# Block sums of the second weight matrix made by loads that add to SBUF, two VectorE additions in place of four

## The chip, the cores and the metric

One core of one Trainium2 chip. The metric is the device time of one execution in microseconds, the median of several runs. TensorE (PE) multiplies, with weight loads (PEld) beside the products; VectorE (DVE), ScalarE (ACT) and GpSimd (POOL) work element by element; SyncE (SP) and GpSimd issue most DMAs. Each engine takes its instructions in order.

## The reference

The kernel computes a block of a transformer on `x` of 2048 tokens by 512 channels: a linear attention, added to `x`, and then a token-mixing MLP, added again:

```python
x = A_x
h = x + _A_ref(_layernorm(x), A_wqkv, A_w_phi, A_wo)
# _B_ref(z), with z = layernorm(h); S = 2048, D = 512, F = 1792
u = gelu(einsum("bsd,sf->bdf", layernorm(z), w1) + b1)
y = einsum("bdf,fs->bds", u, w2) + b2
h2 = h + y.transpose(0, 2, 1)
```

The change lies in the second MLP product, `y`, with `w2` of 1792 by 2048 in float32.

## The kernel before, in words

The attention and the first MLP product (`w1`, weights split in a high and a low float32r part, lines 663 and 670, three products each, lines 66 to 68) end at about 375 us. The second product runs from there to the end.

It is done by blocks with a scheme of the Strassen kind: each 256 by 256 block of `w2` and the matching block of U are cut in 2 by 2, and 7 products of sums of sub-blocks replace 8. The sums on U's side (`operands_u`) are made once and kept in `UB`; those on the side of the weights are made as the weights stream in.

- A *step* is one pair of output tiles `sp` (0 to 7) and one block row `p` (0 to 6); there are 56 steps in the order of `STEPS`, 7 to a pair. `pair_of_tiles(sp, p)` issues the products of a step: `wide` (lines 921 and 924) and `narrow` (line 913).
- A *group* is two steps (`GRP`), 28 in all. For each there is a tile `wraw` with 7 slots of 128 columns a step. Two DMAs from SyncE (line 852), one a step, 256 KB each, fill slots 0 to 3 with the four sub-blocks. Four VectorE operations (lines 854 to 857) put the sums in slots 4, 5, 0 and 6. There are four such tiles in turn: a group's load waits until the group four before it has been split.
- `w2_parts` splits the seven slots: ScalarE writes the high part `whi`, VectorE the low part `wlo` (line 875). There are three such pairs of tiles, so the parts of group g wait for the steps of group g - 3.
- `in_order` fixes the program's order on VectorE, ScalarE and TensorE as it is written; it adds no waits. `stream_w2(n)` runs behind step n and every second step issues the parts of the group two ahead and the sums of the group four ahead. Behind the next to last step of a pair nothing is issued; it comes behind the pair's last step instead, after that step's end sums.
- At the last step of a pair, the products are in six PSUM banks: `b16`, `b7`, `b5`, `b4`, which the next pair writes again, and `b3`, `b2`, which alternate with another two. ScalarE and VectorE (lines 979 to 989) sum them into `ot` and `low`. GpSimd then issues three accumulating stores of 256 KB into `out`: two from `ot` (line 991), and one from `low` (line 992) into rows that the second also adds to, so it waits for that one to land.
- The first five groups are loaded, and two split, while the first product still runs (from 266.9 us).

The table `P1` to `P7` names for each of the 7 products the slot of the weights and the operand of U.

Of the kernel before, what the change touches and what calls it, by code (L numbers as in the profile page):

```python
# [12 lines left out]
ALU = mybir.AluOpType  # L13
# [4 lines left out]
P = 128  # L18
# [19 lines left out]
def block_kernel(ctx: ExitStack, tc: tile.TileContext, x, xT, wT, phic, wo, w1, b1, w2, b2,  # L38
                 kvmask, ident_in, out):
    nc = tc.nc  # L40
# [18 lines left out]
    def split(hi, lo, src, lo_engine):  # L59

        nc.scalar.activation(hi, src, AF.Copy)
        lo_engine.tensor_sub(lo, src, hi)
# [15 lines left out]
    sums = wqp.tile([P, SUMS, NPR, 2, 2], F32, name="smq")  # L78
# [576 lines left out]
    w2v = w2.rearrange("(k p) s -> p k s", p=P)  # L655
# [125 lines left out]
    NP = NF // 2  # L781
# [52 lines left out]
    STEPS = [(sp, p) for sp in range(NT // 2) for p in range(NP)]  # L834
    GRP = 2
    AW, RAW = {}, {}
    QUEUE = {}

    def in_order(*ops):

        for op in ops:
            with ExitStack() as st:
                for ins in QUEUE.values():
                    st.enter_context(tc.issue_after(ins))
                ins = op().ins
            QUEUE[ins.engine] = ins

    def w2_sums(g):
        other = g > AHEAD + 2 and g % 4 == 1
        raw = RAW[g] = (hp if other else ws).tile([P, GRP, 7, P], F32, name="wraw", bufs=1 if other else 3)  # L850
        for i, (sp, p) in enumerate(STEPS[g * GRP:(g + 1) * GRP]):
            nc.sync.dma_start(raw[:, i, 0:4].rearrange("p (k i) s -> p k (i s)", k=2),
                              w2v[:, 2 * p:2 * p + 2, sp * 2 * P:(sp + 1) * 2 * P])
        sums = (lambda: nc.vector.tensor_add(raw[:, :, 4], raw[:, :, 0], raw[:, :, 2]),
                lambda: nc.vector.tensor_sub(raw[:, :, 5], raw[:, :, 4], raw[:, :, 1]),
                lambda: nc.vector.tensor_sub(raw[:, :, 0], raw[:, :, 1], raw[:, :, 0]),
                lambda: nc.vector.tensor_sub(raw[:, :, 6], raw[:, :, 3], raw[:, :, 5]))
        if g < AHEAD:
            with tc.issue_after(LO[-18]):
                for op in sums:  # L860
                    op()
        else:
            in_order(*sums)

    def w2_parts(g):
        home = hp if g % 3 == 2 else ws
        wh_ = home.tile([P, GRP, 7, P], F32R, name="whi")
        wl_ = home.tile([P, GRP, 7, P], F32R, name="wlo")
        for i, step in enumerate(STEPS[g * GRP:(g + 1) * GRP]):
            AW[step] = wh_[:, i], wl_[:, i]  # L870
        raw = RAW.pop(g)
        if g < AHEAD:
            split(wh_, wl_, raw, nc.vector)
        else:
            in_order(lambda: nc.scalar.activation(wh_, raw, AF.Copy), lambda: nc.vector.tensor_sub(wl_, raw, wh_))  # L875

    AHEAD = 2
    for g in range(AHEAD):
        w2_sums(g)
        w2_parts(g)  # L880
    for g in range(AHEAD, AHEAD + 2):
        w2_sums(g)
    parts_next, sums_next = [], []

    def stream_w2(n):

        if (n + 1) % NP == 0:
            for g in sums_next:
                w2_sums(g)
            sums_next.clear()  # L890
        if n % GRP == 0:
            parts_next.append(n // GRP + AHEAD)
        if (n + 2) % NP == 0:
            return
        for g in parts_next:
            if g * GRP < len(STEPS):
                w2_parts(g)
            if (g + 2) * GRP < len(STEPS):
                if (n + 3) % NP == 0:
                    sums_next.append(g + 2)  # L900
                else:
                    w2_sums(g + 2)
        parts_next.clear()


    P1, P2, P3, P4, P5, P6, P7 = (1, 1), (3, 3), (6, 2), (2, 6), (4, 4), (5, 5), (0, 0)

    def narrow(o, ps, m, sp, opens, closes):

# [20 lines left out]
    def new_bank(pool):  # L930
        return pool.tile([P, 2, HD], F32, name="py", tag="pu")

    def pair_of_tiles(sp, p):
        t = 2 * sp
        if p == 0:
            b3, b2 = [new_bank((ps_f, ps_q)[sp % 2]) for _ in range(2)]
            BK[:] = [new_bank(ps_b) for _ in range(4)] + [b3, b2]
        b16, b7, b5, b4, b3, b2 = BK
        end = p == NP - 1
        if t + 2 == NT:  # L940
            if p < NP - 3 or end:
                ps = [p - 2, p - 1, p] if end else [p]
                places = [(b16[:, 0], P1, True), (b16[:, 1], P6, False), (b7[:, 0], P7, True), (b5[:, 0], P5, True),
                          (b4[:, 0], P4, True), (b3[:, 0], P3, True), (b2[:, 0], P2, True)]
                for o, m, opens in places if end else places[5:] + places[:5]:
                    narrow(o, ps, m, sp, opens, True)
                if end:
                    last_sums(t, HB)
            return
        w3, w2, w7, w5, w4 = (b3, P3), (b2, P2), (b7, P7), (b5, P5), (b4, P4)  # L950
        if p == 0:
            wide(sp, p, w3, w2)
        elif not end:
            wide(sp, p, w3, w2, w7, w5, w4)
        narrow(b16[:, 0], [p], P1, sp, True, True)
        narrow(b16[:, 1], [p], P6, sp, False, True)
        if p == 0:
            wide(sp, p, w7, w5, w4)
        if not end:
            return  # L960
        wide(sp, p, w7)
        wide(sp, p, w5, w4)
        wide(sp, p, w3, w2)
        e = uo.tile([P, 2, HD], F32, name="e")
        u2 = uo.tile([P, HD], F32, name="u2", bufs=1)
        u3 = uo.tile([P, HD], F32, name="u3")
        ot = uo.tile([P, 2, 2, HD], F32, name="ot", bufs=1)
        low = hp.tile([P, 2, HD], F32, name="low")
        l5 = hp.tile([P, HD], F32, name="l5")

        def tile_sum(i, k, o, add):
            return lambda: nc.vector.scalar_tensor_tensor(ot[:, i, k], o, b2s[:, t + i:t + i + 1], add,  # L972
                                                          op0=ALU.add, op1=ALU.add)

        def low_sum(o, a):
            return lambda: nc.vector.tensor_add(o, a[:, 1], o)


        in_order(lambda: nc.scalar.activation(e[:, 1], b16[:, 0], AF.Copy),
                 lambda: nc.scalar.activation(l5, b5[:, 1], AF.Copy),  # L980
                 lambda: nc.vector.tensor_add(u2, b16[:, 1], e[:, 1]),
                 lambda: nc.vector.tensor_add(u3, b7[:, 0], u2), low_sum(u3, b7),
                 tile_sum(0, 1, b4[:, 0], u3),
                 lambda: nc.vector.tensor_add(l5, b5[:, 0], l5),
                 low_sum(ot[:, 0, 1], b4),
                 lambda: nc.vector.tensor_add(e[:, 0], l5, u2),
                 lambda: nc.scalar.activation(low[:, 0], b3[:, 1], AF.Copy),
                 lambda: nc.scalar.activation(low[:, 1], b2[:, 1], AF.Copy),
                 tile_sum(0, 0, l5, u3), tile_sum(1, 0, b3[:, 0], e[:, 0]), tile_sum(1, 1, b2[:, 0], e[:, 1]))
        for i in range(2):  # L990
            nc.gpsimd.dma_start(out[(t + i) * P:(t + i + 1) * P, :], flat(ot[:, i]), accum_op=ALU.add)  # L991
        nc.gpsimd.dma_start(out[(t + 1) * P:(t + 2) * P, :], flat(low), accum_op=ALU.add)
# [9 lines left out]
    def last_sums(t, hb):  # L1002
        b16, b7, b5, b4, b3, b2 = BK
        e = uo.tile([P, 2, HD], F32, name="e")
        u2 = uo.tile([P, HD], F32, name="u2", bufs=1)
        u3 = uo.tile([P, HD], F32, name="u3")
        add = nc.vector.tensor_add
        nc.scalar.activation(e[:, 1], b16[:, 0], AF.Copy)
        in_order(lambda: add(u2, b16[:, 1], e[:, 1]),
                 lambda: add(hb[1][:, 0], u2, hb[1][:, 0]),  # L1010
                 lambda: add(hb[1][:, 1], e[:, 1], hb[1][:, 1]),
                 lambda: add(u3, b7[:, 0], u2),
                 lambda: add(hb[0], hb[0], u3.unsqueeze(1).to_broadcast([P, 2, HD])),
                 lambda: add(hb[0][:, 0], b5[:, 0], hb[0][:, 0]),
                 lambda: add(hb[1][:, 0], b5[:, 0], hb[1][:, 0]),
                 lambda: add(hb[0][:, 1], b4[:, 0], hb[0][:, 1]))
        nc.sync.dma_start(out[t * P:(t + 1) * P, :], flat(hb[0]))
        for k, o, q in ((0, b3, nc.scalar), (1, b2, nc.sync)):
            in_order(lambda: add(hb[1][:, k], o[:, 0], hb[1][:, k]))
            q.dma_start(out[(t + 1) * P:NT * P, k * HD:(k + 1) * HD], hb[1][:, k])  # L1020
# [54 lines left out]
```

## Time and profile before

| what | us |
|---|---|
| median of 3 runs | 519.54 (519.3 to 520.09) |
| span of the profiled execution, first to last instruction | 517.9 |
| TensorE busy | 513.2 (99%) |
| VectorE busy | 395.0 (76%) |
| ScalarE busy | 285.3 (55%) |
| GpSimd busy | 235.9 (46%) |
| second product, from the first `py` product to the end | 375.5 to 517.9 |

The span lies 1.6 us below the median; no other time of the profiled execution is on its page. The granted TensorE clock is 1.00 throughout. How to read rows: a timeline row has start, duration, engine, line, operation, `out<-in`, and in brackets the idle time before it and what ended it. Rows of a tile have minimum, median and maximum in ns. "To landing" is the time from a DMA's issue to its last byte's arrival. Busy times of TensorE overlap from one product to the next, so starts are what is compared.

### The profile page before, as it was taken

The numbers are of one execution on the slowest core, as the hardware profiler recorded it, in microseconds if no ns is written. First come the engines' busy times: TensorE is split into PE (matmuls) and PEld (weight loads), VectorE is DVE, ScalarE is ACT, GpSimd is POOL, SyncE is SP. The second block draws the span as 40 slices with busy tenths as digits, with TensorE's granted clock in tenths as the row PEclk, the third lists the DMA queues.
The fourth block names the chain that finished last, engine by engine and source line by source line (L and its number), as shares of the span: only waits on it lengthen the run. The fifth ranks groups of instructions, "written<-read, shape, count | busy, mean of one in ns | idle before, by whom it ended". The sixth has DMA issues, their size and how long they took to land.

```text
span 517.9 us, 9772 instructions
## 1 busy us (share of the span) xinstructions
PE 513.2 (99%) x3761; PEld 434.0 (84%) x3761; DVE 395.0 (76%) x719; ACT 285.3 (55%) x501; POOL 235.9 (46%) x182
## 2 busy tenths in 40 slices
PE   9999999999999999999999999999999999999997
PEld 8888888888887777777788888888899999999997
DVE  6799889989987899697336624625797899888993
ACT  6999853526267877767756423425464434433530
POOL 3579997876999999974224000000001102110210
PEclk9999999999999999999999999999999999999999
DMA  8642301021302334333255433532134586557732
GB/s 311 209 142 84 102 22 42 1 83 44 122 27 97 103 103 119 107 103 123 82 163 162 123 94 90 184 102 62 41 115 94 141 201 136 139 156 181 137 48 61
DMA packets 46493, 57.66 MB, mean 111 GB/s; under 512 B 4080, under 2 KB 33136, under 8 KB 46448
## 3 DMA queue, kind: packets, MB, share of 16 engines
q1 hardware_dynamic: 43136, 51.38, 31.4%
q0 software_dynamic: 3024, 5.51, 7.6%
q8 instruction: 29, 0.48, 0.4%
q10 hardware_dynamic: 288, 0.17, 0.1%
q14 instruction: 16, 0.13, 0.1%
HBM read 46.81 MB, written 10.22 MB: 110 GB/s over the span
## 4 chain that ended last, share of the span: by engine, by line
PE 97%; DVE 1%; ACT 1%; issue 0%; DVEq 0%
PE pu L66 13%; PE pu L68 12%; PE pu L67 12%; PE py L921 11%; PE py L913 10%; PE py L924 6%; PE po L66 3%; PE pk_ps L66 3%; PE po L68 3%; PE po L67 3%; PE pk_ps L67 3%; PE pk_ps L68 3%; PE pv L67 3%; PE pv L66 3%; PE pv L68 3%; PE tr L591 2%
## 5 line engine op out<-in xcount | busy, mean ns | idle before, releaser
L991 POOL DMA_DIRECT2D out<-ot x14 | 12.5, 941 | 170.3 <-DVE ot L972 170.3
L66 PE MATMUL pu<-hs,whi 128*128 128x512 f32 x224 | 87.7, 394 | 0.0
L67 PE MATMUL pu<-hs,whi 128*128 128x512 f32 x224 | 87.2, 389 | 0.0
L68 PE MATMUL pu<-hs,wlo 128*128 128x512 f32 x224 | 86.5, 389 | 0.0
L670 DVE TENSOR_TENSOR wlo<-wraw,whi 128x512 fp32r<-128x512 f32 x56 | 46.9, 841 | 46.5 <-ACT whi L663 46.2
L875 ACT ACTIVATE whi<-wraw 128x1792 fp32r<-128x1792 f32 x26 | 44.0, 1704 | 30.9 <-issue 17.4
L663 ACT ACTIVATE whi<-wraw 128x512 fp32r<-128x512 f32 x56 | 34.6, 625 | 44.4 <-PE pu L67 39.4
L875 DVE TENSOR_TENSOR wlo<-wraw,whi 128x1792 fp32r<-128x1792 f32 x26 | 52.4, 2019 | 0.0
L66 PEld LDWEIGHTS pu<-hs,whi 128*128 128x128 f32 x224 | 42.0, 188 | 9.1 <-ACT hj L641 0.2
L68 PEld LDWEIGHTS pu<-hs,wlo 128*128 128x128 f32 x224 | 42.0, 188 | 8.9
L67 PEld LDWEIGHTS pu<-hs,whi 128*128 128x128 f32 x224 | 42.1, 188 | 8.5
L921 PE MATMUL py<-uf,whi 128*128 128x512 f32 x175 | 48.4, 395 | 0.0
L484 POOL TENSOR_TENSOR ez<-eq,zB 128x1024 f32<-128x1024 f32 x16 | 38.4, 2405 | 3.8 <-ACT zB L544 3.8
L913 PE MATMUL py<-uf,whi 128*128 128x256 f32 x210 | 39.0, 283 | 0.0
L213 POOL TENSOR_TENSOR pk<-pk,sk 128x1024 f32<-128x1024 f32 x16 | 31.1, 1949 | 11.2 <-DVE sk L212 10.0
L508 POOL TENSOR_TENSOR eq<-eq,w 128x1024 f32<-128x1024 f32 x16 | 32.4, 2026 | 3.2 <-DVE w L505 3.2
L921 PEld LDWEIGHTS py<-uf,whi 128*128 128x128 f32 x175 | 30.1, 189 | 3.9
L913 PEld LDWEIGHTS py<-uf,whi 128*128 128x128 f32 x210 | 32.8, 192 | 0.0
L217 POOL TENSOR_TENSOR zacc<-zacc,pk 128x1024 f32<-128x1024 f32 x13 | 31.4, 2412 | 0.5
L924 PEld LDWEIGHTS py<-uf,wlo 128*128 128x128 f32 x175 | 27.1, 189 | 3.8
L913 PE MATMUL py<-uf,wlo 128*128 128x256 f32 x105 | 29.7, 283 | 0.0
L924 PE MATMUL py<-uf,wlo 128*128 128x256 f32 x175 | 28.7, 281 | 0.0
(200 smaller groups left out, 1303.9 us busy)
## 6 DMA issues: line engine op xcount, KB each, us to landing
wraw<-in_w SPq DMA_DIRECT2D x112, 256.0 KB, 3.0
xraw<-in_xT SPq DMA_DIRECT2D x16, 256.0 KB, 2.9
xh<-in_x SPq DMA_DIRECT2D x16, 256.0 KB, 2.6
h<-in_x SPq DMA_DIRECT2D x16, 256.0 KB, 2.7
out<-h SPq DMA_DIRECT2D x16, 256.0 KB, 2.1
out<-ot POOLq DMA_DIRECT2D x14, 256.0 KB, 4.4
wraw<-in_wT SPq DMA_DIRECT2D x12, 256.0 KB, 5.1
out<-low POOLq DMA_DIRECT2D x7, 256.0 KB, 4.2
```

The lines of the kernel that those rows point to most:

```text
L66: nc.tensor.matmul(o, ah, bh, start=first, stop=False)
L67: nc.tensor.matmul(o, ah, bl, start=False, stop=False)
L68: return nc.tensor.matmul(o, al, bh, start=False, stop=last).ins
L217: nc.gpsimd.tensor_add(zacc, zacc, PK[t])
L484: nc.gpsimd.tensor_mul(EZ[t], EQ[t], zB)
L508: nc.gpsimd.tensor_mul(heads(EQ[t]), heads(EQ[t]), W[t].rearrange("p g c h -> p (g c h)").unsqueeze(2).to_broadcast([P, 2 * H, DH]))
L663: nc.scalar.activation(wh_, raw, AF.Copy)
L670: LO.append(nc.vector.tensor_sub(wl_, raw, wh_).ins)
L875: in_order(lambda: nc.scalar.activation(wh_, raw, AF.Copy), lambda: nc.vector.tensor_sub(wl_, raw, wh_))
L913: in_order(lambda: nc.tensor.matmul(o, x[:, m[0]], UB[p, m[1]][:, y], start=opens and p == 0 and i == 0, stop=closes and p == NP - 1 and i ...
L921: in_order(lambda: nc.tensor.matmul(o, wh_[:, m[0]], UB[p, m[1]], start=p == 0, stop=False, skip_group_check=True))
L924: in_order(lambda: nc.tensor.matmul(o[:, 0], wl_[:, m[0]], UB[p, m[1]][:, 0], start=False, stop=p == NP - 1, skip_group_check=True))
```

## The change

Slots are used differently: the four sub-blocks go to slots 1 to 4 (one DMA a step), and a second plain DMA copies the third of them (64 KB a step) to slot 0. When both have landed, GpSimd issues for each step a DMA that adds 128 columns by two of `w2` (128 KB) to slots 0 and 1. Two of the block sums come about in this way. VectorE makes the other two (slots 5 and 6), both additions. Some products thereby have the opposite sign, and the end sums subtract where they added. `w2_load(g)` is split from `w2_sums(g)`: loads are issued for the group five ahead of the current step's group, sums now directly before the parts of the group ahead of them. The number and shapes of TensorE's products stay as they are.

```diff
-    def w2_sums(g):
+    def w2_load(g):
+        if g * GRP >= len(STEPS):
+            return
         other = g > AHEAD + 2 and g % 4 == 1
         raw = RAW[g] = (hp if other else ws).tile([P, GRP, 7, P], F32, name="wraw", bufs=1 if other else 3)
         for i, (sp, p) in enumerate(STEPS[g * GRP:(g + 1) * GRP]):
-            nc.sync.dma_start(raw[:, i, 0:4].rearrange("p (k i) s -> p k (i s)", k=2),
-                              w2v[:, 2 * p:2 * p + 2, sp * 2 * P:(sp + 1) * 2 * P])
-        sums = (lambda: nc.vector.tensor_add(raw[:, :, 4], raw[:, :, 0], raw[:, :, 2]),
-                lambda: nc.vector.tensor_sub(raw[:, :, 5], raw[:, :, 4], raw[:, :, 1]),
-                lambda: nc.vector.tensor_sub(raw[:, :, 0], raw[:, :, 1], raw[:, :, 0]),
-                lambda: nc.vector.tensor_sub(raw[:, :, 6], raw[:, :, 3], raw[:, :, 5]))
+            cols = sp * 2 * P
+            nc.sync.dma_start(raw[:, i, 1:5].rearrange("p (k i) s -> p k (i s)", k=2),
+                              w2v[:, 2 * p:2 * p + 2, cols:cols + 2 * P])
+            nc.sync.dma_start(raw[:, i, 0], w2v[:, 2 * p + 1, cols:cols + P])
+        for i, (sp, p) in enumerate(STEPS[g * GRP:(g + 1) * GRP]):
+            cols = sp * 2 * P
+            nc.gpsimd.dma_start(raw[:, i, 0:2].rearrange("p i s -> p (i s)"), w2v[:, 2 * p, cols:cols + 2 * P],
+                                accum_op=ALU.add)
+
+    def w2_sums(g):
+        if g * GRP >= len(STEPS):
+            return
+        raw = RAW[g]
+        sums = (lambda: nc.vector.tensor_add(raw[:, :, 5], raw[:, :, 0], raw[:, :, 2]),
+                lambda: nc.vector.tensor_add(raw[:, :, 6], raw[:, :, 4], raw[:, :, 5]))
...
     AHEAD = 2
+    for g in range(AHEAD + 1):
+        w2_load(g)
     for g in range(AHEAD):
         w2_sums(g)
         w2_parts(g)
-    for g in range(AHEAD, AHEAD + 2):
-        w2_sums(g)
-    parts_next, sums_next = [], []
+    for g in range(AHEAD + 1, AHEAD + 3):
+        w2_load(g)
+    w2_sums(AHEAD)
+    parts_next = []
 
     def stream_w2(n):
 
-        if (n + 1) % NP == 0:
-            for g in sums_next:
-                w2_sums(g)
-            sums_next.clear()
         if n % GRP == 0:
             parts_next.append(n // GRP + AHEAD)
         if (n + 2) % NP == 0:
             return
         for g in parts_next:
+            w2_sums(g + 1)
             if g * GRP < len(STEPS):
                 w2_parts(g)
-            if (g + 2) * GRP < len(STEPS):
-                if (n + 3) % NP == 0:
-                    sums_next.append(g + 2)
-                else:
-                    w2_sums(g + 2)
+            w2_load(g + 3)
         parts_next.clear()
 
-    P1, P2, P3, P4, P5, P6, P7 = (1, 1), (3, 3), (6, 2), (2, 6), (4, 4), (5, 5), (0, 0)
+    P1, P2, P3, P4, P5, P6, P7 = (2, 1), (4, 3), (6, 2), (3, 6), (0, 4), (5, 5), (1, 0)
...
-                 lambda: nc.vector.tensor_add(u2, b16[:, 1], e[:, 1]),
-                 lambda: nc.vector.tensor_add(u3, b7[:, 0], u2), low_sum(u3, b7),
+                 lambda: nc.vector.tensor_sub(u2, b16[:, 1], e[:, 1]),
+                 lambda: nc.vector.tensor_sub(u3, u2, b7[:, 0]),
+                 lambda: nc.vector.tensor_sub(u3, u3, b7[:, 1]),
...
```

The remaining lines change the same signs in `tile_sum` and in `last_sums`. By the order of the built program, GpSimd's queue in the second product is: accumulating loads of groups 3 to 8, stores of pair 0, groups 9 to 11, pair 1, 12 to 15, pair 2, 16 to 18, pair 3, 19 to 22, pair 4, 23 to 25, pair 5, 26 and 27, pair 6. In the first product, the accumulating loads of groups 0 to 2 stand between the operations of `operands_u` (lines 804 to 807) for `p` of 0 and 1.

More of the change, by code (lines that the diff above doesn't have):

```diff
@@ L969, in pair_of_tiles, with tile_sum @@
         l5 = hp.tile([P, HD], F32, name="l5")
-        def tile_sum(i, k, o, add):
+        def tile_sum(i, k, o, add, op=ALU.add):
             return lambda: nc.vector.scalar_tensor_tensor(ot[:, i, k], o, b2s[:, t + i:t + i + 1], add,
-                                                          op0=ALU.add, op1=ALU.add)
+                                                          op0=ALU.add, op1=op)
         def low_sum(o, a):
@@ L988, in pair_of_tiles @@
                  lambda: nc.scalar.activation(low[:, 1], b2[:, 1], AF.Copy),
-                 tile_sum(0, 0, l5, u3), tile_sum(1, 0, b3[:, 0], e[:, 0]), tile_sum(1, 1, b2[:, 0], e[:, 1]))
+                 tile_sum(0, 0, l5, u3), tile_sum(1, 0, b3[:, 0], e[:, 0], ALU.subtract), tile_sum(1, 1, b2[:, 0], e[:, 1]))
         for i in range(2):
@@ L1006, in last_sums @@
         u3 = uo.tile([P, HD], F32, name="u3")
-        add = nc.vector.tensor_add
+        add, sub = nc.vector.tensor_add, nc.vector.tensor_sub
         nc.scalar.activation(e[:, 1], b16[:, 0], AF.Copy)
-        in_order(lambda: add(u2, b16[:, 1], e[:, 1]),
-                 lambda: add(hb[1][:, 0], u2, hb[1][:, 0]),
+        in_order(lambda: sub(u2, b16[:, 1], e[:, 1]),
+                 lambda: sub(hb[1][:, 0], hb[1][:, 0], u2),
                  lambda: add(hb[1][:, 1], e[:, 1], hb[1][:, 1]),
-                 lambda: add(u3, b7[:, 0], u2),
+                 lambda: sub(u3, u2, b7[:, 0]),
                  lambda: add(hb[0], hb[0], u3.unsqueeze(1).to_broadcast([P, 2, HD])),
                  lambda: add(hb[0][:, 0], b5[:, 0], hb[0][:, 0]),
-                 lambda: add(hb[1][:, 0], b5[:, 0], hb[1][:, 0]),
+                 lambda: sub(hb[1][:, 0], hb[1][:, 0], b5[:, 0]),
                  lambda: add(hb[0][:, 1], b4[:, 0], hb[0][:, 1]))
```

## The prediction

> **What bounds the kernel now.** I read the page from the top: engines, chain, queues.
>
> ```profile
> PE 513.2 (99%) x3761; PEld 434.0 (84%) x3761; DVE 395.0 (76%) x719; ACT 285.3 (55%) x501; POOL 235.9 (46%) x182
> PE 97%; DVE 1%; ACT 1%; issue 0%; DVEq 0%
> q1 hardware_dynamic: 43136, 51.38, 31.4%
> q0 software_dynamic: 3024, 5.51, 7.6%
> wraw<-in_w SPq DMA_DIRECT2D x112, 256.0 KB, 3.0
> out<-ot POOLq DMA_DIRECT2D x14, 256.0 KB, 4.4
> out<-low POOLq DMA_DIRECT2D x7, 256.0 KB, 4.2
> ```
>
> TensorE is busy 513.2 of 517.9 us and holds 97% of the chain. A change that leaves its instructions alone, as this one does, can gain only where TensorE waits, so I looked for waits in the second product with the view by stretches. One row is one pair of output tiles (7 steps); the columns are PE, PEld, DVE, ACT, POOL, clock, DMA share, GB/s.
>
> ```profile
> 414.98:432.28 17.30, 17.30 (x115) 15.77 (x114) 15.95 (x31) 6.43 (x7) 2.61 (x3) 1.00 0.70 165
> 432.28:449.58 17.30, 17.30 (x115) 15.77 (x114) 15.50 (x26) 8.02 (x8) 2.61 (x3) 1.00 0.61 140
> ```
>
> VectorE is at 15.5 to 15.95 of 17.30 us, nearly full, but TensorE has no gap at all: 17.30 of 17.30. VectorE's load is a risk that does not bite yet. What the change saves there has no wait to shorten; what it makes later has to be compared with the room that is left.
>
> **What it removes.** The timelines of VectorE and TensorE around the end of a pair:
>
> ```profile
> 413.10 2.02 DVE L875 TENSOR_TENSOR wlo<-wraw,whi 128x1792 fp32r<-128x1792 f32 x1
> 415.03 0.42 DVE L854 TENSOR_TENSOR wraw<-wraw 128x256 f32<-128x256 f32 x1
> 415.49 0.42 DVE L855 TENSOR_TENSOR wraw<-wraw 128x256 f32<-128x256 f32 x1
> 415.83 0.42 DVE L856 TENSOR_TENSOR wraw<-wraw 128x256 f32<-128x256 f32 x1
> 416.51 2.02 DVE L875 TENSOR_TENSOR wlo<-wraw,whi 128x1792 fp32r<-128x1792 f32 x1
> 423.31 2.02 DVE L875 TENSOR_TENSOR wlo<-wraw,whi 128x1792 fp32r<-128x1792 f32 x1
> 426.31 0.42 DVE L981 TENSOR_TENSOR u<-py,e 128x256 f32<-128x256 f32 x1 [0.99 <-ACT e L979]
> 415.08 1.32 PE L921 MATMUL py<-uf,whi 128*128 128x512 f32 x5
> 416.24 0.76 PE L924 MATMUL py<-uf,wlo 128*128 128x256 f32 x5
> 428.15 0.40 PE L913 MATMUL py<-un,whi 128*128 128x256 f32 x2
> 431.06 0.76 PE L924 MATMUL py<-un,wlo 128*128 128x256 f32 x5
> ```
>
> Four sums start 415.03 and the next operation 416.51: 1.48 us a group. Two take 0.46 + 0.34 = 0.80, so VectorE is relieved of 0.68 us in each of the 28 groups, 19 us. On the path that sets the end: 0, for the reason above. The sums behind each pair (L981 and after) keep their number; some additions become subtractions, costed at nothing, since the row's form (128x256, two operands) stays.
>
> **What it moves.** The listing of VectorE's order shows a group's two sums now directly ahead of the low parts of the group before. At the ends of pairs 1, 3 and 5 the low parts of group 8 (15, 22) come right behind the end sums: 413.10 to 415.12, first read by TensorE at 416.24, 1.12 us to spare. With 0.80 of sums ahead of it 0.3 is left: no stall, if group 9 is there by then.
>
> **What it adds: a chain for each group.** Before, a load landed and VectorE could begin. Now SyncE issues four loads instead of two, GpSimd waits for them, issues two accumulating loads (one a step, 128 KB, 128 rows of 1 KB), and only then come the sums. GpSimd issues in order, and in its queue stand the three accumulating stores of each pair, the third waiting for the first two to land:
>
> ```profile
> 412.69 1.74 POOL L991 DMA_DIRECT2D out<-ot  x2 [9.27 <-DVE ot L972]
> 419.57 0.86 POOL L992 DMA_DIRECT2D out<-low  x1 [5.13 <-DMA out<-ot]
> 429.99 1.75 POOL L991 DMA_DIRECT2D out<-ot  x2 [9.55 <-DVE ot L972]
> 415.15 0.98 SPq L852 DMA_DIRECT2D wraw<-in_w  x2
> L992 POOL DMA_DIRECT2D out<-low x7: 856/865/867, 402.6 to 505.6; - x7
> L991 POOL DMA_DIRECT2D out<-ot x14: 858/958/1171, 395.4 to 499.9; - x14
> DMA to landing us min/median/max: 2.5/3.1/5.7
> DMA to landing us min/median/max: 3.8/4.4/6.0
> DMA to landing us min/median/max: 3.8/4.2/4.9
> ```
>
> (The last three are the views of the tiles wraw, ot and low.) From the first store at 412.69 GpSimd is taken until 419.57 + 0.86 = 420.43; whatever accumulating load is queued behind stands for 7.7 us. By the listing that is groups 12 and 13, 19 and 20, 26 and 27 behind stores 1, 3, 5, and in the other pairs groups 9, 16, 23.
>
> Group 12 is the tight one. Its buffer is that of group 8, free at about 415.9; two issues span 0.98 us, four take about 2, and they land by 420.4 (415.9 + 1.5 + 3.0): in time for GpSimd at 420.43. The second accumulating load is issued at 420.43 + 0.87 = 421.3 and lands La later. Then VectorE needs 0.80 for sums(12) and 1.93 (413.10 to 415.03) for the low parts of group 11, which stand behind them: those end at 424.03 + La instead of 425.33. TensorE reads them at 431.06, so that alone costs nothing. But next on VectorE are the end sums of pair 2 (before: 426.31), whose first, 0.42 long, must read bank b16 before pair 3 overwrites it at 428.15. It may start at 427.73 at the latest. **Stall at this place = La + X - 3.7 us**, X being how much later than before the third store is issued. The same order recurs at the ends of pairs 4 and 6.
>
> La: no row shows an accumulating load into SBUF. From below, a plain load of twice the bytes: 3.0 median, 2.5 at best. From above, the slowest accumulating store of twice the bytes: 6.0. I take the stores' 4.2, nearest in queue, in number of rows and in operation; half the bytes speak for less, the crowding below for more. With X = 0 the stall is 0.5 a place, 1.5 in all. The pairs between follow by the same steps: group 11's low parts end at 428.2, group 15 is loaded 4.5 us later and its second accumulating load issued by 433.6; store 2 starts there, its third part 6.9 us later at 440.5; GpSimd is free at 441.4, and group 16's second load goes out at 442.2 and lands at 446.4, 1.3 us before its sums are due at 413.10 + 2 x 17.30 = 447.7. The crowding below can use that up; I leave it to the upper half of the range.
>
> Crowding: queue q1 spends 31.4% of 517.9 us on 51.38 MB, 3.16 us/MB; q0 7.6% on 5.51 MB, 7.14 us/MB. A pair now has a DMA share of 0.61 to 0.70, 11.3 us of 17.3. The change adds 7 copies of 64 KB (0.46 MB x 3.16 = 1.5 us) and 7 accumulating loads of 128 KB (0.92 x 7.14 = 6.5 us): 19.3 us of 17.3. Partly this counts waiting, so I do not take it as a bound yet, but nearly every transfer will meet another. What meeting costs, the spreads of the rows show: 4.9 against 4.2 for one store, 6.0 against 4.4 for the pair before it. So La = 4.9 and X = 1.6: 2.8 us a place, **8.4 us** for three.
>
> The Trainium skill, DMA: Bandwidth & Descriptors, section on the anatomy of a GpSimd-issued DMA, gives such a DMA about 2.0 us plus its bytes over 436 GB/s; that is an estimate of 2.3 us for 128 KB, by which the stall would be nil, the first of the rivals below. For the 256 KB stores it would say 2.6, and the trace has 4.2 and 4.4, so the row is used.
>
> **The first product.** The early loads, and six accumulating loads that GpSimd has between the operands of U, come at 267 to 280 us.
>
> ```profile
> 274.83 0.74 POOL L807 TENSOR_TENSOR tt<-u,tt 128x256 f32<-128x256 f32 x1
> 279.24 0.95 DVE L62 TENSOR_TENSOR un<-tt,un 128x768 fp32r<-128x768 f32 x1
> 276.56 0.69 DVE L670 TENSOR_TENSOR wlo<-wraw,whi 128x512 fp32r<-128x512 f32 x1
> 280.35 0.39 PE L66 MATMUL pu<-hs,whi 128*128 128x512 f32 x1
> 280.57 0.39 PE L67 MATMUL pu<-hs,whi 128*128 128x512 f32 x1
> ```
>
> Five issues of 0.87 come ahead of L807: up to 4.4 us later; its reader on VectorE came 3.7 us after it ended. The low weights then ready at 277.25 are read at 280.57, 3.3 us on. So 0; if the cover fails, 1 to 2 us.
>
> **The sum.** Removed 0, moved 0, added 8.4 against an execution of 517.9 us span; the median of 519.54 has 1.6 more around it, taken as unchanged: 519.54 + 8.4 = 527.9.
>
> **The rivals.** *The cover holds* (not slower): an accumulating load lands like a plain one, La = 3.0, and the stores are no later. Then 3.0 - 3.7 is below 0, TensorE stays at 17.30 of 17.30, and the time is 519.5. For it: half the bytes of the rows that I used. Against: the crowding. It decides at La + X = 3.7 us; beyond it each us costs 3. *The DMA engines become the bound*: 19.3 - 17.3 = 2.0 us a pair over some 6.5 pairs, 13 us, 532.5; should a row of 1 KB cost as much as one of 2 KB, the accumulating loads need 13.1 us a pair and the excess of 8.6 gives 575. For it the two rates; against it, that the stores' rate contains waiting. The Trainium skill, DMA: Bandwidth & Descriptors, section "Issuing engines are not separate DMA queues", says that transfers from all queues run on the same 16 DMA engines and interleave, which is this rival's premise; the rows here, at a share of 0.70 at most, do not show them full. *VectorE's relief speeds TensorE* (faster): five L921 take 1.16 us (415.08 to 416.24), 0.232 each, against about 0.22 (280.35 to 280.57) for the same form in the first product. If all of these some 10 ns hung on VectorE, 0.68 x 3.5 = 2.4 of its 15.7 us gone would return a sixth of 49 x 5 x 10 ns = 2.5 us: 0.4 us, less than the measurement can tell.
>
> **How the numbers follow.** The measurement tells about 0.2%, 1.04 us, from no change. Forecast (stalls at three pair ends, 521 to 532) 0.55; DMA-bound 0.27, of which 0.05 lies far out; cover holds 0.15; anything faster 0.03. Slower 0.82, same 0.15, faster 0.03. The range goes from 519.2, half of the case of no change, to 542, which takes in the DMA-bound case but for its far end.
>
> **What would show it.** Right: TensorE's idle time sits at steps 21, 35 and 49, in front of L913 on bank b16, released by VectorE; VectorE waits for DMA in front of the sums of groups 12, 19 and 26; accumulating loads land in 4 to 5 us; the stores' third issue is later than 6.9 us after the first. Wrong: no idle time on TensorE after 375 us (the cover held), stalls spread over all groups with a DMA share near 1 (DMA-bound), or idle time at 267 to 300 us.

## The result, and the profile after

The changed kernel takes 541.9 us (median of 4 runs, 540.87 to 543.03) against 519.75 us for the kernel before, measured beside it: ratio 1.0427, 95% interval 1.0412 to 1.0443. It is 22.2 us slower. The forecast was 527.9 us, 8.4 us slower, in a range of 519.2 to 542.0.

Rows of the page of the changed kernel: engines, granted clock by slices, DMA queues, and four groups of DMAs with their median time from issue to landing.

```profile
PE 521.3 (97%) x3761; PEld 439.8 (81%) x3761; DVE 377.0 (70%) x663; ACT 285.9 (53%) x501; POOL 285.2 (53%) x238
PEclk9999999999999999999999999999999979979989
q1 hardware_dynamic: 51200, 55.05, 32.8%
q0 software_dynamic: 11088, 12.85, 16.4%
wraw<-in_w SPq DMA_DIRECT2D x112, 256.0 KB, 3.6
wraw<-in_w POOLq DMA_DIRECT2D x56, 128.0 KB, 5.3
out<-ot POOLq DMA_DIRECT2D x14, 256.0 KB, 5.7
```

The span is 540.0 us. VectorE has given up 18 us of work (395.0 to 377.0), as the change says. TensorE issues the same 3761 products but is busy 8.1 us longer: the clock row has dips in slices 33, 36 and 39, where it had none before. Queue q0 holds 16.4% of the DMA engines instead of 7.6%: 16.4% of 540.0 less 7.6% of 517.9 is 49.2 us for 56 adding loads, 0.88 us of all 16 engines each, with the stores' part taken as unchanged.

The waits of TensorE, and then of VectorE, in the second product (total us, times, longest us):

```profile
PE py L920 <- DVE u L988: 13.6, 3, 5.6
PE py L920 <- DVE l L992: 0.2, 1, 0.2
```

```profile
DVE wraw L867 <- DMA wraw<-in_w: 24.5, 3, 9.2
```

There are three waits of TensorE for bank b16, released by the first end sum of a pair, and three waits of VectorE for a DMA ahead of a group's sums. TensorE's lie at steps 21, 35 and 49 (5.61, 5.33 and 2.63 us), the ends of pairs 2, 4 and 6. The timeline around the first, GpSimd, VectorE and TensorE in turn:

```profile
412.14 0.86 POOL L860 DMA_DIRECT2D wraw<-in_w  x1 [2.58 <-DVE l L992]
413.86 0.86 POOL L860 DMA_DIRECT2D wraw<-in_w  x1 [0.85 <-DMA wraw<-in_w]
414.40 2.13 POOL L999 DMA_DIRECT2D out<-ot  x2
422.87 0.86 POOL L1000 DMA_DIRECT2D out<-low  x1 [6.34 <-ACT whi L886]
423.55 2.00 POOL L860 DMA_DIRECT2D wraw<-in_w  x2
...
431.41 0.43 DVE L867 TENSOR_TENSOR wraw<-wraw 128x256 f32<-128x256 f32 x1 [9.17 <-DMA wraw<-in_w]
432.21 2.02 DVE L886 TENSOR_TENSOR wlo<-wraw,whi 128x1792 fp32r<-128x1792 f32 x1
434.15 0.42 DVE L988 TENSOR_TENSOR u<-py,e 128x256 f32<-128x256 f32 x1
...
434.62 0.80 PE L920 MATMUL py<-un,whi 128*128 128x256 f32 x2 [5.61 <-DVE u L988]
436.07 1.66 PE L928 MATMUL py<-un,whi 128*128 128x512 f32 x3
438.17 2.33 PE L928 MATMUL py<-un,whi 128*128 128x512 f32 x5
```

The chain can be read from top to bottom. The two loads of group 11 stand ahead of the stores, so the first store starts at 414.40. The third store goes out at 422.87, the loads of group 12 behind it. The second of those starts at about 424.5 and has landed only when VectorE starts the sums at 431.41. The low parts of group 11 follow, then the end sum at 434.15 that lets TensorE go on at 434.62. The last row shows something else: five products of 512 columns take 2.33 us, against 1.32 for the same form before. By stretches (us, busy time and instructions of PE, PEld, DVE, ACT, POOL, then the granted clock, DMA share, GB/s):

```profile
411.00:428.00 17.00, 17.00 (x111) 15.33 (x110) 10.86 (x17) 8.14 (x8) 7.50 (x9) 1.00 0.98 195
434.00:436.00 2.00, 1.38 (x6) 1.38 (x7) 1.77 (x5) 0.07 (x1) 0.00 (x0) 0.50 0.62 139
436.00:438.00 2.00, 2.00 (x8) 1.48 (x7) 2.00 (x7) 0.00 (x0) 0.27 (x1) 0.50 0.72 231
438.00:440.00 2.00, 2.00 (x7) 1.61 (x7) 1.97 (x4) 0.75 (x1) 1.53 (x3) 0.50 0.37 59
440.00:442.00 2.00, 2.00 (x15) 1.86 (x14) 1.97 (x4) 0.95 (x1) 1.73 (x2) 0.85 0.79 94
```

After the wait TensorE works at half clock until past 440 us. And the DMA engines, at a share of 0.70 before, are taken for 0.98 of the stretch of 411 to 428.

Landing times, from the views of the tiles wraw, ot and low (min, median, max us):

```profile
DMA to landing us min/median/max: 2.3/4.5/8.4
DMA to landing us min/median/max: 3.9/5.7/8.0
DMA to landing us min/median/max: 3.7/5.5/7.0
```

### The profile page after: what moved, and what is told of

Same layout as the page of the kernel before. It is cut to its first block, busy times and chain, and to the rows that moved or that the text cites. A ratio compares the mean times of both kernels' runs of the same rounds, so it can differ in the third digit from the quotient of the medians.

```text
span 540.0 us, 10038 instructions
## 1 busy us (share of the span) xinstructions
PE 521.3 (97%) x3761; PEld 439.8 (81%) x3761; DVE 377.0 (70%) x663; ACT 285.9 (53%) x501; POOL 285.2 (53%) x238
## 3 DMA queue, kind: packets, MB, share of 16 engines
q0 software_dynamic: 11088, 12.85, 16.4%
## 5 line engine op out<-in xcount | busy, mean ns | idle before, releaser
L860 POOL DMA_DIRECT2D wraw<-in_w x56 | 51.3, 1139 | 136.8 <-DMA wraw<-in_w 71.6
L867 DVE TENSOR_TENSOR wraw<-wraw 128x256 f32<-128x256 f32 x28 | 11.7, 419 | 34.2 <-DMA wraw<-in_w 33.8
L920 PE MATMUL py<-un,whi 128*128 128x256 f32 x84 | 18.9, 319 | 13.9 <-DVE u L988 13.6
```

Source lines behind the costliest of these rows:

```text
L860: nc.gpsimd.dma_start(raw[:, i, 0:2].rearrange("p i s -> p (i s)"), w2v[:, 2 * p, cols:cols + 2 * P], accum_op=ALU.add)
L920: in_order(lambda: nc.tensor.matmul(o, x[:, m[0]], UB[p, m[1]][:, y], start=opens and p == 0 and i == 0, stop=closes and p == NP - 1 and i ...
```

## The experiments

The theory: the time is lost where the sums of a group wait on VectorE for late adding loads, ahead of the end sums that free a bank. The rivals: the order on VectorE is enough by itself; the bytes in the DMA engines are enough by themselves; the third store, which holds GpSimd's queue, is the whole of it.

### The order on VectorE, and the adding

**e1_sums_behind_ends**: the sums of groups 5, 12, 19 and 26 go behind the end sums of their pairs, as in the kernel before.

```diff
-    parts_next = []
+    parts_next, sums_next = [], []
...
+        if (n + 1) % NP == 0:
+            for g in sums_next:
+                w2_sums(g)
+            sums_next.clear()
...
-            w2_sums(g + 1)
+            if (n + 3) % NP == 0:
+                sums_next.append(g + 1)
+            else:
+                w2_sums(g + 1)
```

> The sums of groups 5, 12, 19 and 26 stand behind the end sums of pairs 0, 2, 4 and 6 on VectorE instead of ahead of them; all loads as in the changed kernel. Queue theory (a late accumulating load holds up the end sums through VectorE's fixed order, and TensorE then waits for bank b16): the three waits of 5.6, 5.3 and 2.6 us in front of the first narrow product go, and with them the stretches of half clock behind them; 520 to 525 us. Rival, DMA engines full: the same bytes have to move, the parts come late all the same and TensorE waits for them instead; 533 us or more.

530.45 us, ratio 1.0213 (1.0193 to 1.0233): about half comes back. No wait for b16 is left; others take their place. TensorE's and ScalarE's waits, and two rows of the timelines of GpSimd and ScalarE:

```profile
PE py L935 <- ACT whi L886: 5.8, 2, 3.3
```

```profile
ACT low L1002 <- DMA out<-low: 13.6, 4, 6.3
```

```profile
446.33 0.86 POOL L1007 DMA_DIRECT2D out<-low  x1 [8.42 <-DMA wraw<-in_w]
450.71 0.38 ACT L1002 ACTIVATE low<-py 128x256 f32<-128x256 f32 x1 [5.61 <-DMA out<-low]
```

The third store of pair 2 goes out at 446.33, its first at 435.78; the second takes 9.4 us to land. There is one tile `low`, so ScalarE's copy for pair 3 waits until that store has landed, at 450.71. Behind the copy on ScalarE stand the high parts of the next weights, and TensorE waits for those. The lateness has found another way to TensorE.

**e8_before_early_sums**: the kernel before, with that one order of the changed kernel.

```diff
-                if (n + 3) % NP == 0:
-                    sums_next.append(g + 2)
-                else:
-                    w2_sums(g + 2)
+                w2_sums(g + 2)
```

> The kernel before, with one thing of the changed one: the sums of groups 5, 12, 19 and 26 are not put behind the end sums of their pairs, but stand in their place ahead of them (loads by SyncE alone, no adding loads, four sums a group). If that order is enough to make the waits, banks are released late here too: 525 us or more, waits at steps 21, 35 and 49 for VectorE. If it needs the late adding loads, this stays within 1 us of 519.8.

520.2 us against 519.69 beside it, ratio 1.0009 (0.9999 to 1.0018). VectorE is nearly full in the stretch before the start of step 21, and TensorE is full before and after, and in the stretch where step 35 starts:

```profile
411.00:428.00 17.00, 17.00 (x112) 15.52 (x112) 16.73 (x30) 7.77 (x8) 2.60 (x3) 1.00 0.76 165
428.00:445.00 17.00, 17.00 (x111) 15.25 (x110) 13.89 (x25) 6.15 (x7) 2.60 (x3) 1.00 0.69 146
462.00:479.00 17.00, 17.00 (x110) 15.30 (x109) 13.89 (x26) 6.29 (x7) 2.62 (x3) 1.00 0.71 161
```

So the order alone costs nothing that can be told; it only passes on what is late.

**e3_plain_loads** and **e4_small_adds**: GpSimd's loads write instead of adding; or add 32 columns instead of 256. The edit of the first:

```diff
-            nc.gpsimd.dma_start(raw[:, i, 0:2].rearrange("p i s -> p (i s)"), w2v[:, 2 * p, cols:cols + 2 * P],
-                                accum_op=ALU.add)
+            nc.gpsimd.dma_start(raw[:, i, 0:2].rearrange("p i s -> p (i s)"), w2v[:, 2 * p, cols:cols + 2 * P])
```

> GpSimd's 56 loads into SBUF overwrite instead of adding (the two block sums that they make are left out); queue, order, number and bytes as in the changed kernel. Queue theory: what matters is the wait in GpSimd's queue; a plain load lands perhaps 1 us earlier, so the three waits shrink by about 1 us each; 536 to 540 us. Rival, DMA engines full because adding costs them twice: share of the DMA engines falls by some 0.2 and the waits go; 520 to 526 us.

> Each accumulating load adds 32 columns of 256 only (an eighth of the bytes, the same 128 rows; most of the two block sums is left out). Queue theory: GpSimd's queue is the same, the loads land 1 to 2 us earlier; waits of 3 to 4 us stay; 532 to 538 us. Rival, DMA engines full: they are relieved by some 0.25 of their time, the waits go; 520 to 525 us.

532.1 us, ratio 1.0244 (1.021 to 1.0278), and 532.14 us, ratio 1.0237 (1.022 to 1.0254). The waits of TensorE in the one and the other:

```profile
PE py L919 <- DVE u L987: 8.3, 3, 3.7
```

```profile
PE py L920 <- DVE u L988: 6.0, 3, 3.0
```

The three places stay and the waits shorten. GpSimd's plain loads land in 3.4 us (median), the adding ones in 5.3. The adding costs 9.8 us; a load through GpSimd that adds nothing costs the other 12.4. With an eighth of the bytes added, as much comes back as with no adding, so the cost is that of adding 128 KB at a time.

**e5_order_and_plain**: e1's and e3's edits together.

> The changed kernel with both edits that each gave back about half: the sums of groups 5, 12, 19 and 26 behind the end sums of their pairs, and GpSimd's loads writing instead of adding (two block sums are left out). If the two are separate causes (order on VectorE, and the time an adding load takes to land), their gains add: 541.9 less 11.5 less 9.8 = 520.6, with no wait over 1 us in the second product. If both act on the same wait (the adding load's lateness, which the order only passes on), one takes what the other leaves or less: 525 to 530 us.

521.15 us, ratio 1.0024 (1.0012 to 1.0036). The gains add up (541.9 - 11.5 - 9.8 = 520.6). ScalarE's wait for the third store, 13.6 us in e1, has shrunk too:

```profile
ACT low L1001 <- DMA out<-low: 3.9, 2, 2.7
```

### The bytes

**e6_loads_by_sync**: the same 56 loads of 128 KB, issued by SyncE.

```diff
-            nc.gpsimd.dma_start(raw[:, i, 0:2].rearrange("p i s -> p (i s)"), w2v[:, 2 * p, cols:cols + 2 * P],
-                                accum_op=ALU.add)
+            nc.sync.dma_start(raw[:, i, 5:7].rearrange("p i s -> p (i s)"), w2v[:, 2 * p, cols:cols + 2 * P])
```

> The same 56 extra loads of 128 KB, but by SyncE's queue, writing, into places that nothing else writes before the sums (5 and 6, so that no load waits for another); two block sums are left out. Bytes through the DMA engines are those of the changed kernel or its plain-load form; GpSimd's queue carries stores only, as before; the order on VectorE is the changed kernel's. If the chain through GpSimd's queue (place behind the stores, landing of an adding load) is the cause, the waits at steps 21, 35 and 49 go: 519.5 to 522 us. If the DMA engines' load as such is the cause, loads land late here too: 528 to 535, with waits of TensorE for the sums or for low parts.

519.97 us, ratio 1.0007 (0.9997 to 1.0016). Two of its stretches, with the DMA share in the column before the last:

```profile
428.00:445.00 17.00, 17.00 (x112) 15.51 (x112) 11.81 (x19) 6.09 (x7) 2.60 (x3) 1.00 1.00 267
462.00:479.00 17.00, 17.00 (x111) 15.47 (x111) 11.83 (x19) 6.42 (x7) 2.62 (x3) 1.00 0.95 251
```

There are more bytes per second here than in the changed kernel, at a share of 0.95 to 1.00, and TensorE never waits. The bytes of plain loads are harmless if the loads are issued in time. With two sums a group on VectorE, as in the changed kernel, it is no faster than before either.

**e9_adds_unread**: the adding loads go to a tile that nothing reads.

```diff
+    spare = ur.tile([P, 4, HD], F32, name="u").rearrange("p (a i) d -> p a i d", a=2)
+    nc.gpsimd.memset(spare, 0.0)
...
-            nc.gpsimd.dma_start(raw[:, i, 0:2].rearrange("p i s -> p (i s)"), w2v[:, 2 * p, cols:cols + 2 * P],
-                                accum_op=ALU.add)
+            nc.gpsimd.dma_start(spare[:, g % 2, i], w2v[:, 2 * p, cols:cols + 2 * P], accum_op=ALU.add)
```

> The changed kernel, with GpSimd's 56 adding loads going to a tile that nothing reads, so that no sum waits for them (they leave two block sums out, as the plain loads did; the first of them wait until that tile is free, near the end of the first product). Instructions, bytes, and GpSimd's queue in the second product are the changed kernel's. If the adding loads cost time by what waits for them, all the loss goes: 519.5 to 521.5 us. If they cost time by their work in the DMA engines (49 us of them over the kernel, which delays SyncE's loads), 525 us or more, with waits for low parts.

530.55 us, ratio 1.0206 (1.0191 to 1.0221): the number of the second case. The stretches say why it doesn't settle the question:

```profile
428.00:445.00 17.00, 15.34 (x99) 13.41 (x98) 10.41 (x15) 5.75 (x6) 10.36 (x13) 1.00 1.05 208
445.00:462.00 17.00, 11.01 (x56) 9.16 (x55) 8.78 (x16) 5.59 (x7) 10.32 (x12) 0.80 0.99 200
462.00:479.00 17.00, 17.00 (x109) 15.17 (x109) 12.80 (x20) 7.06 (x8) 2.59 (x3) 1.00 0.94 217
```

With no load of SyncE's to wait for, all 56 loads went out between 362.8 and 459 us, 0.58 a us; in the changed kernel the 46 of the second product take 133 us, 0.35 a us. From 394 us on and while they last, SyncE's loads land in 8.1 to 10.3 us (medians of stretches of 17 us; all loads into that tile in the changed kernel 5.2 to 6.4), the stores come late, and TensorE waits. The waits end with the last of these loads. The run measured another rate than the one in question, and another order: adding loads stand between the two `ot` stores of a pair (stores at 415.08 and 417.62, a load at 417.08).

**e13_adds_unread_paced**: the same, with a one-column copy on GpSimd ahead of each load.

```diff
...
+            nc.gpsimd.tensor_copy(spare[:, i, 0:1], raw[:, i, 0, 0:1])
+            nc.gpsimd.dma_start(spare[:, i], w2v[:, 2 * p, cols:cols + 2 * P], accum_op=ALU.add)
```

> As e9_adds_unread (GpSimd's adding loads go to a tile that nothing reads; two block sums left out), but paced as in the changed kernel: a one-column copy on GpSimd ahead of each makes it wait for SyncE's load of its group, and the tile is filled at the start. So the adding loads, their rate and their places between the stores are the changed kernel's, and only the sums' wait for them is gone. If the loss comes through the sums that wait, 519.5 to 522 us. If the adding loads delay SyncE's loads or the stores at this rate too, 525 to 531 us, and the waits name low parts, high parts or the copies that the third store holds.

566.15 us, ratio 1.0893 (1.0863 to 1.0924). GpSimd's waits show that the copy itself made a worse chain: it waits for the load into the same tile a group earlier, and holds the stores.

```profile
POOL spare L863 <- DMA spare<-in_w: 34.1, 24, 3.8
```

It says nothing on the question.

**e14_adds_unread_between_stores**: e9 again, with the order of loads and stores on GpSimd fixed, 6 or 8 loads after the stores of each pair.

```diff
-            nc.gpsimd.dma_start(spare[:, g % 2, i], w2v[:, 2 * p, cols:cols + 2 * P], accum_op=ALU.add)
+            in_order(lambda: nc.gpsimd.dma_start(spare[:, g % 2, i], w2v[:, 2 * p, cols:cols + 2 * P], accum_op=ALU.add))
...
```

> As e9_adds_unread (the adding loads go to a tile that nothing reads, two block sums left out), with the 40 last adding loads fixed between the stores in GpSimd's queue, 6 or 8 a pair, so that they run at the changed kernel's mean rate (0.4 a us) and not at 0.58. Nothing that GpSimd's queue waits for is added. If the loss comes through the sums that wait for the adding loads, 519.5 to 522 us. If the adding loads at this rate also delay the low parts, the high parts or the stores, 524 us or more.

521.01 us, ratio 1.0037 (1.0015 to 1.0059). Stretches and the only wait of TensorE:

```profile
411.00:428.00 17.00, 17.00 (x112) 15.48 (x111) 14.42 (x22) 7.89 (x9) 7.69 (x9) 1.00 1.05 207
428.00:445.00 17.00, 17.00 (x112) 15.48 (x111) 11.80 (x19) 5.49 (x5) 9.15 (x11) 1.00 1.13 265
```

```profile
PE py L933 <- DVE wlo L888: 0.2, 1, 0.2
```

The same adding loads go out at a like rate (the last 40 in 97 us, 0.41 a us), the DMA engines are full, GpSimd's third store comes 6.5 to 9.6 us behind the first, and 1.1 us is lost. So at this rate the work of the adding loads in the DMA engines costs about 1 us. The other 21 of the 22 us come through waits: what waits for the adding loads, and what stands in GpSimd's queue behind them while they wait for SyncE's loads. The run leaves out both, and doesn't tell them apart.

### The third store

**e2_store_elsewhere** sends it to other rows, so that it waits for neither of the first two; **e10_order_and_store** adds e1's order to that.

```diff
-        nc.gpsimd.dma_start(out[(t + 1) * P:(t + 2) * P, :], flat(low), accum_op=ALU.add)
+        other = (t - 1) % NT
+        nc.gpsimd.dma_start(out[other * P:(other + 1) * P, :], flat(low), accum_op=ALU.add)
```

> The third accumulating store of each pair goes to the rows of the tile before the pair, where nothing is under way, so it doesn't wait for the first two to land; number and bytes of all transfers stay, and the output's rows are wrong. Queue theory: GpSimd is free some 6 us earlier at the end of each pair, the accumulating loads of groups 12, 19 and 26 go out that much earlier, and the three waits of TensorE go; 520 to 524 us. Rival, DMA engines full: the same bytes at the same time, little changes; 535 us or more.

> Two edits together: the sums of groups 5, 12, 19 and 26 behind the end sums of their pairs (530.5 alone), and the third store of a pair to the rows of an earlier tile, so that it waits for neither of the first two (537.2 alone; half of two tiles' output then goes to other rows). If what is left with the order alone is GpSimd held at the third store, the two together return to 520 to 522 us. If it is the landing of an adding load by itself (4.8 us median), 527 to 531 us.

537.15 us, ratio 1.0339 (1.0285 to 1.0392): 4.7 us come back, and the 520 to 524 us of the queue theory are missed. But the run moves the lateness more than it removes it. At the end of pair 1 all three stores now start within 1.1 us (from 414.01), and SyncE's loads of group 12, issued behind them from 416.36 on, take 7.7 to 8.2 us to land, against 5.5 to 5.9 in the changed kernel. GpSimd is free at 417.02, waits for them, and issues its first adding load of group 12 at 425.57, 2.0 us later than in the changed kernel. So the run doesn't price that wait by itself. With the order, 525.79 us, ratio 1.0115 (1.0075 to 1.0155), against 530.45 for the order alone; that lies between the two cases of its expectation.

**e12_no_third_store** drops it and lets VectorE add the 512 columns; **e11_order_no_third_store** adds e1's order.

```diff
+                 lambda: nc.vector.tensor_add(ot[:, 1], ot[:, 1], low))
...
-        nc.gpsimd.dma_start(out[(t + 1) * P:(t + 2) * P, :], flat(low), accum_op=ALU.add)
```

> The changed kernel with the third store replaced by VectorE's addition, and nothing else: the sums stand where the change put them. With the third store's waiting but not its data gone the time was 537.2; if its 256 KB and descriptors delay the adding loads behind it as well, 530 to 536 us; if only the order on VectorE and the landing matter, 535 to 541 us, with waits at steps 21, 35 and 49 as before.

> The sums behind the end sums, and no third store: its 512 columns are added to the second tile's sums by VectorE (one addition a pair, about 0.6 us) before that tile's store. Seven stores of 256 KB and their wait go. If the third store and its queueing hold the adding loads, 520 to 523 us. If the adding loads are late without it too, 526 to 531 us.

531.99 us, ratio 1.024 (1.0223 to 1.0256), and 523.08 us, ratio 1.0067 (1.005 to 1.0084). The waits of TensorE in e12 and in e11:

```profile
PE py L920 <- DVE u L988: 5.6, 3, 2.8
PE py L931 <- DVE wlo L886: 0.8, 3, 0.3
```

```profile
PE py L938 <- DVE wlo L886: 1.0, 3, 0.4
PE py L927 <- DVE wlo L886: 0.5, 1, 0.5
```

The third store with its 256 KB is worth 9.9 us in the changed order and 7.4 with the other: it delays the adding loads behind it (without it the first one of group 12 goes out at 420.55 instead of 423.55), and holds ScalarE's copies. e11, the fastest form that still adds in the load and computes the whole reference, is 3.4 us behind the kernel before. Nothing here beats that kernel: its TensorE has no wait to lose.

### The clock

**e7_filled_waits**: while it would wait, TensorE does the first products of steps 21, 35 and 49 again.

```diff
         if p == 0:
-            wide(sp, p, w3, w2)
+            for _ in range(8 if sp in (3, 5) else 1):
+                wide(sp, p, w3, w2)
...
-                for o, m, opens in places if end else places[5:] + places[:5]:
+                for o, m, opens in places if end else places[5:] * (4 if p == 0 else 1) + places[:5]:
```

> The changed kernel, with the first products of steps 21, 35 and 49 done again before the waits (each begins its bank anew, so the repeats change nothing): 7 repeats of four products at steps 21 and 35, 3 of six at step 49, so that TensorE works through about 5.5, 5.5 and 2.4 us of its waits of 5.6, 5.3 and 2.6 us. If the products run at half clock after a wait because TensorE stood idle, the clock stays near 1.00 here and about 7 us of the 22 come back: 534 to 536 us, with the releases at the old times. If the slow clock comes from something else (the DMA load in those stretches, the time), it stays: 541 to 543 us.

536.7 us, ratio 1.0329 (1.0312 to 1.0346), a little above the first case: 5.2 us come back by doing more work.

```profile
434.00:436.00 2.00, 1.56 (x8) 1.00 (x8) 1.88 (x6) 0.00 (x0) 0.00 (x0) 1.00 0.59 182
436.00:438.00 2.00, 2.00 (x11) 1.61 (x11) 1.97 (x7) 0.00 (x0) 0.86 (x1) 1.00 0.48 145
438.00:440.00 2.00, 2.00 (x16) 1.87 (x15) 2.00 (x2) 1.50 (x1) 1.86 (x3) 1.00 0.54 81
```

The clock stays at 1.00 in the stretches that had 0.50. The bank was released at about the old time (TensorE went on at 433.87 at step 21, against 434.62). So the half clock comes from TensorE's idleness, and it is a cost of its own. The 5.2 us don't measure that cost exactly: at step 21 TensorE went on 0.75 us earlier, and at step 35 the repeats ran some 1.2 us past the release.

## Why the prediction was off in size

The measured 541.9 us lies 0.1 us inside the range, and that is luck: the range went so far for the case that the DMA engines become the bound, and the loss came another way. The forecast itself, 8.4 us slower, was too small by a factor of 2.6.

**What held.** The direction, the places and the mechanism are those of the forecast: three waits in front of the first product on b16, released by VectorE, VectorE in turn waiting for a DMA ahead of the sums of groups 12, 19 and 26. The first product lost nothing. VectorE's relief brought nothing (e6). The rate of the DMA engines came out as worked out: 7 adding loads a pair take 7 x 0.88 = 6.2 us (6.5 in the forecast), and their share did go to about 1. The pair ends between, of pairs 1, 3 and 5, were costed at 0, and TensorE doesn't wait there.

**The term La + X - 3.7.** This was mis-sized. At step 21, La was 6.9 us (about 424.5 to 431.41), taken as 4.9; X was 3.3 us (third store at 422.87 instead of 419.57), taken as 1.6. The term gives 6.9 + 3.3 - 3.7 = 6.5; TensorE had come to that point 0.7 us later than before, which leaves 5.8, and it waited 5.61. The form was right, the inputs were not. La was read from stores as they ran in a DMA share of 0.7, plus their small spread, and at a share of 0.98 both the stores (median 5.7 instead of 4.4) and the new loads went further out. Of X, 1.6 us is that same slowing. The other 1.7 us is the first store's start, 414.40 instead of 412.69: 0.6 of it was there long before the second product, and 1.1 I had left out, as the loads of group 11 stand ahead of the stores and the second waits for SyncE's load. The third store wasn't alone in the way either. The forecast had SyncE's loads of group 12 landed by 420.4; they were issued at 416.80 to 418.40 and landed at 422.7 to 423.9, about when GpSimd came free for the first adding load (423.55). Had the third store waited less and its bytes still moved, these loads would have held the adding loads to about the same time, as they did in e2; without the store (e12) they landed at 419.7 to 420.8. In all the waits are 13.6 us where the forecast had 8.4.

**A missing term: the clock.** "2.8 us a place" counted waits at their length. After each, TensorE ran at half clock; by the granted clock in stretches of 1 us that costs 3.0, 1.9 and 1.7 us, 6.6 in all, and e7 gives back 5.2. The Trainium skill, TensorE: Matmul & The Clock Gate, Part 1, says that the clock falls to half after an idle window of some 3.4 us, and that these windows run free of the program; by that rule a wait of 2.8 us, shorter than a window, would have had no price beyond its length. The trace agrees on the window, in that the slow stretches last 3.4 us or twice that, and differs on the idle time that it takes, as the wait of 2.63 us was enough. 13.6 and 6.6 make 20.2 of the 22.2 us. Of the other 2.0, 0.6 is no effect of the change: TensorE lost it at 6 to 7 us, where the changed kernel's profile has 7 products and the other 11. The rest lies in pieces under 0.7 us, which no run here takes apart.

**The rivals.** "The DMA engines become the bound" was right on the share and wrong on its price: e6 and e14 run with the engines as full and lose 0.3 and 1.1 us. A share near 1, which the prediction named as a sign for that case, shows nothing alone. At 0.58 adding loads a us, in another order, other loads landed in 8 to 10 us and TensorE did wait (e9). "The cover holds" failed because an adding load landed in 5.3 us (median) and not in 3.0; with plain loads by GpSimd it still needs the other order (e5), and with plain loads by SyncE it holds in the changed order (e6).

## What to carry to other kernels

Work taken off an engine that nobody waits for is worth nothing, while the DMA that replaces it adds a link to a chain; price that link in its queue, with everything ahead of it and with the DMA share that the change itself will make, not with the landing times of the quieter kernel. When an in-order engine must wait for such a link, look at what stands behind it: here moving two additions behind the end sums, at four pair ends, was worth as much as not adding at all. And a forecast wait of some 1.6 us or more on TensorE is to be priced with the slow stretch that may follow it: here 1.7 to 3.0 us each.

## What the runs showed of the hardware

- An adding load of 128 KB into SBUF, issued by GpSimd, lands in 5.3 us (median) where a writing one takes 3.4 (e3). It takes 0.88 us of all 16 DMA engines, the writing one 0.48 (12.4% of 533.0 us less the same 39.4 us, over 56).
- Half clock followed waits much shorter than 3.4 us: 1.60 us at step 21 of e4 and 2.52 us in e1, while 1.89 us at step 21 of e3 and waits of 1.26 to 1.49 us in e10 left the clock at 1.00.
- The granted clock changes on a grid of 3.41 us. By the trace's record of it, the slow stretches of the changed kernel begin at 433.77, 474.73 and 519.10 us, the later two 12 and 25 steps after the first, and last two, two and one step; those of the second product in e1, e2, e3, e4 and e12 also begin a whole number of steps apart (11 to 13) and last one or two. So where a wait falls on the grid matters: the 1.60 us of e4 fell within one step, the 1.89 us of e3 into two (1.24 and 0.64). How much idle time in a step it takes is not settled here.
- The slow stretch begins up to 5 us after the wait does (the third wait of the changed kernel ends at 517.03, with the clock at 1.00 until 519 and at 0.50 from 520 to 522), so a wait may be paid for by products that come well after it.
- Stretches with a DMA share of 0.95 to 1.13 went by without any wait of TensorE (e6, e14).
